# A four-layer attention kernel: the last layer's last block attends with block-diagonal operands on TensorE, and the order is searched anew

## The chip, the cores and the metric

The kernel runs on one core of a Trainium2 chip. The metric is the device time of one execution in microseconds; lower is better. Besides the times there is one profiled execution, whose trace lists every instruction of TensorE (PE, with its weight loads as PEld), VectorE (DVE), ScalarE (ACT), GpSimd (POOL) and the DMA issues of SyncE (SP).

## The reference

The input is `x` of 2048 tokens by 512 channels, in bf16. Four residual layers follow one another, A, B, A, B, with the same weights for both A and for both B layers. Each normalizes `x`, attends with 32 heads of 16 channels, projects and adds to `x`.

```python
def _A_ref(x, wqkv, w_phi, wo):                 # linear attention
    ...
    phi_q = jnp.concatenate([_softmax(pq, axis=-1), _softmax(-pq, axis=-1)], axis=-1)
    phi_k = jnp.concatenate([_softmax(pk, axis=-1), _softmax(-pk, axis=-1)], axis=-1)
    kv = jnp.einsum("bhsf,bhsd->bhfd", phi_k, v)
    ...
def _B_ref(x, wqkv, wo):                        # dilated window
    W, dil = 8, 2
    ...
    idx = pos[:, None] - off[None, :]           # off = 0, 2, ..., 14
    ...
    logits = jnp.einsum("bhsd,bhswd->bhsw", q, kg) * scale
    logits = jnp.where(mask[None, None, :, :], logits, -1e9)
    attn = _softmax(logits, axis=-1)
    o = jnp.einsum("bhsw,bhswd->bhsd", attn, vg)
...
x = x + _A_ref(_layernorm(x, axis=-1), ...)
x = x + _B_ref(_layernorm(x, axis=-1), ...)
x = x + _A_ref(_layernorm(x, axis=-1), ...)
x = x + _B_ref(_layernorm(x, axis=-1), ...)
```

In a B layer a token attends to itself and to the seven tokens 2, 4, ..., 14 places before it. Even tokens therefore see even tokens only, and odd ones odd.

## The kernel before

The tokens are cut into four blocks `b` of 512, and each block into four tiles `t` of 128. `x` stays in SBUF for all four layers (`x_83` to `x_86` in the profile are blocks 0 to 3). A class `_Fast` holds one method per stage; a method does not issue instructions but appends steps (closures) to threads, one thread for each stage and engine.

What sets the order of all engines is a list written out in the file: `_ORDER` names one thread after another, and `run` takes the next step of that thread. So the order of each engine's instructions is fixed by hand (by a search done beforehand), and each engine runs its own list strictly in order. `_CHOICE` has one bit for each PSUM eviction or similar step that could run on DVE or ACT (`flex`): 1 puts it on DVE. `_SLOTS` gives for each buffer that is asked for the slot it gets: 8 `big` ones (8 KB per partition), 16 `med`, 6 `t2`, and the 8 PSUM banks `ps`. `_OPT` holds options, among them `tr_dma`, the (layer, block) pairs whose normalized `x` is transposed by a DMA rather than by PE.

Stages of an A layer: `s_a1` (keys and values, softmax features, the sum `kv`), `s_a2` (queries), `s_akv`, `s_a3` and `s_a4` (normalization, output, projection with `WoA`, residual). `s_norm` does the normalization; it casts (`xn`, DVE L444 or ACT L446) and transposes (`xnT`, PE L460 with an eviction, or a DMA).

Stages of a B layer, for each block:

- `s_b1`, 48 matmuls 128x512 at L927: queries, keys and values transposed, channels on partitions. The values, with a halo of 16 tokens, are copied by 16 DMAs into `Vg`, which holds shifted copies of them.
- `s_b2`: four DVE products (L1019, `prod`, 128x4096) of the queries with eight shifted views of the keys. 32 matmuls with a 0/1 matrix (L1026, 128x32 tiles) sum them over the channels into logits. ACT takes two exponentials of 128x512 (L1033). Two matmuls (L1042) sum the denominators, ACT inverts them (L1047, L1049), and DVE normalizes (`PT`, L1054).
- `s_b3`: four DVE products (L1081, `pav`, 128x4096) of the probabilities with `Vg`, and 32 matmuls (L1090) that sum them. In the blocks 2 and 3 of the last layer the last product is split into two halves. ACT or DVE evicts to `oT` (L192, L190).
- `s_out`: four 128x512 matmuls per tile with `WoB` (L520), and the residual, added by DVE (L533) or by PE with the identity (L523) and then an ACT copy (L530). In the last layer SP then stores the tile (L544).

At the end `s_flag` counts whether all sums of exponentials (`stE`, 16 columns) and of reciprocals (`stR`, 8 columns) are within bounds. If not, a general path computes everything again.

Of the kernel before, what the change touches and what calls it, by code (L numbers as in the profile page):

```python
# [8 lines left out]
BF16 = mybir.dt.bfloat16  # L9
# [21 lines left out]
VGW = 3 * KVW + TB + 8  # L31
FRO2_MAX = 2.9
# [25 lines left out]
av 8 i i i i i i i i i i i i 0 f 0 g e 2t 0 bs 9 h a d c 0 j k t i i j l 27 o p 3 3 d6 b 1x 1x t 1y o m 2 2 1q  # L58
1z 1x 1x q u t r 1q v x w n s 1r w 1s 4 20 y 21 1x 22 1x 23 1q 1q 1q 1q 1v 1w z 3d 3d 3d 1u 1t 25 3e 3e 3e z 5
3e 3e z z 26 10 18 18 d5 1 z 16 11 4i 15 6 1h 13 3d 3e 3e 25 25 26 18 25 18 12 26 26 28 26 26 26 26 19 12 28  # L60
2a 28 1h 18 14 12 12 1a 28 1c 3e 2g 2g 1f 2h 2h 1h 1h 1b 1i 2b 1b 1e 1d 29 2j 2k 1h 1j 1n 2r 1b 1l 2s 1b 2c 2r
1k 2s 17 2g 2g 2h 2h 1k 1k 2h 2h 2h 2h 2d 1g 2d 2d 2d 2e 2j 1m 35 36 32 2o 2o 33 2s 33 32 33 33 2r 2s 2s 1o 2o
2o 2d 2r 3a 1k 3a 1p 2p 2o 24 24 2s 24 2u 2v 35 37 2u 2u 2u 2s 2i 2w 2j 3a 2s 3a 2l 2z 2j 24 32 32 34 2m 3b 33
3d 3f 3f 2z 2z 2z 33 2f 33 33 2f 2f 2f 3a 3a 2q 2q 2q 30 3a 2n 3a 3a 2z 3e 2q 2x 35 35 b6 3b 3a 2y 31 31 31 31
3c 3c 38 3c 39 3c 3m 3f 3n 3o 3o 3o 24 24 3g 3g 3g 3f 3p 3q 3g 3g 3g 3g 3g 3r 3q 3f 3g 24 3h 3i 3i 5l 5m 5n 3p
3s 3q 3j 3k 3k 3t 3q 3p 3x 5m 3w 3u 3h 3i 3i 3q 3v 3q 3q 3y 3h 3i 3q 3i 3h 3i 3q 5l 5o 5p 5r 5m 5q 7 7 3z 3q
3i 3j 3k 5m 5l 5s 3k 7 7 5m 5m 5m 3h 3i 7g 40 5u 44 41 42 5t 5m 5m 3j 3j 7h 7i 3k 5v 5m 5w 43 7h 45 7j 45 60
3k 3k 3k 46 45 45 5y 5x 5z 61 61 48 47 47 61 49 47 4a 47 4b 62 47 4b 63 3j 4g 94 4c 45 4d 45 4e 4f 3k 45 45 61
64 63 4h 4p 65 95 7j 7j 66 4q 63 96 95 97 97 63 67 7h 63 67 69 7h 6b 4k 4k 4k 4l 4p 4r 4k 4m 4p 4p 4s 4t 7k 7n
6a 68 6c 4o 7m 50 50 4u 4u 4u 4n 4u 7l 4w 97 7o 7p 7p 7q 7s 3l 4x 7r 7r 7p 7t 7p 6o 7u 50 7r 7r 7v 6o 6j 4v 4y  # L70
4j 6o 6q 6o 4j 4z 6k 6p 6r 6j 7r 6e 6l 95 6d 95 7v 6t 6s 6f 6d 7w 6e 7z 7x 98 9b 9a 99 6g 7y 9c 6e 6j 6j 9d 9d
6u 9d 6e 6n 80 6m 9d 6h 6v 6v 9e 9h 9f 6i 9g 9f 6w 6v 6v 6w 6w 9f 9i 9f 87 88 8h 9j 9f 50 82 9j 9l 6w 6x 6x 87
87 6w 81 83 9n 6x 9k 87 8b 89 51 51 51 51 52 52 8c 8c 8e 6u 6u 6u 9m 8j 8a 8d 8c 6v 6y 3l 8f 82 9o 82 85 82 50
51 52 4z 4z 4z 9q 9q 9s 8c 6z 8g 6y 6z 9r 71 70 6y 6y 6z 6z 72 86 a0 a0 a1 73 84 8i 74 75 74 74 50 74 8i 76 8i
77 a2 76 79 53 53 54 55 54 a5 56 53 54 9v 78 76 9q 9q 76 a0 81 53 9v 9w 9p 7a 57 9v 9u a7 76 7a 9t 8j 7c 9y 54
58 59 59 59 9v 59 9x 7d 7e 5a 8j 8j 7b 7f 5c 5b 5d 5b 5b a0 8k 5e 5b 5f 8k 9z a7 5b 5f 5j 8k 8k 8l a3 5i b4 a4
b7 5h b4 b4 b4 8l 5g b5 b5 a7 b5 b5 a7 8k 8l 8j c3 8i c3 b8 c4 c4 c4 c4 a8 8m a8 a8 a8 c3 a9 a9 5k at c1 b5 a6
8m au au c1 c2 b5 c2 aw c2 c2 a8 a9 b5 b5 8n 8o 8n 8p 8m at au at at 8n 8q 8m a7 aa 8n aw 8r 8s au au au 8s 8s
8t au au 8s 8v a6 a6 8u aa 8w aa 8x 8u 8u 8u 8y ab ac ab ad a6 aa b7 8u b9 b7 c3 8y 90 92 c1 91 c1 c2 8z c2 c2
aw ay ab c2 ba ae ab af aw b0 c4 c4 b1 bc ag ag ag ag ah bc aj ak bc c1 c4 c4 bc al ax c3 ai ai ai bd b1 ai am  # L80
93 bf bi bg az bf ai am ar bf bf bg bg aq b7 bg bg bg bg bg bb an ao ag ag ap bi ag ag b1 b1 bc b2 c2 bi bn bi
bl bk as bq br br bq br br bq bq b1 br by by by by bt b3 b3 b3 b3 br be be be br br bz c5 c5 bh bj bn bn bn c5
bu c4 by by by by c6 bo by c6 c6 c5 bt bt bt bn bv c6 c6 c6 bz be bp bp bw bm bp bp c0 c0 by c6 c6 bx c0 c0 c9
c5 ca c6 cb cb cc cb cd ce cd fr fs c7 c8 c7 c8 c8 ft cc ci cf cd cg cd c7 c8 c8 fs fu c8 e2 fu ch cd e3 cd cc
cj ck e4 cd c7 c8 c8 c7 e3 e2 cm cd c8 e6 e7 fu cl cd cd cn cp co e5 e3 hb e3 cr e2 ea e9 cq hc cs e3 cs e8 e3
e3 hd eb ec e3 e3 e3 ed ct cv hc eh cs he ee cs ef cw eg ei cx ei ei cu ei cu cu cu fs cy fs fv ej cu cy d0 cz
ek d2 fw fx fz d3 cs cs fy cs cs g0 g0 g0 el ek em ek en ek d4 d1 dc g1 eo ek g2 g3 g2 dc de eo es g0 g4 dd dh
g2 g5 g2 he hc eq g6 d7 d8 d7 d7 d7 he di dc g2 dc d9 ep er hc et dn hf da db df dh dh dh hi hh hj hg hk hk hk
dj dk dl dm dm g6 g7 g9 dn dn dg ga f0 f0 hl hm hn hm ho hm ev ew f1 hk dn g8 do do hp f2 fa fc hm hq do do dp
ev ex fc gb ev f0 dp ey dn f3 f0 hm fc f4 hq ev ez fc do dp dn dq dq d6 f5 f6 dm dm eu hs gi gj gi fd gs hr fd  # L90
ht fd hu hv fd dq fe fe f5 f5 f8 f5 f9 f7 fb gk fd fe fc gn gn gp gi gi gl gm gd gd gd ge ic gf i7 i7 i9 gg i8
dr dr dt ds dr du hx hy gd dq gu dr dv gn gq gh i7 ff ia gu fb go ff fg fh fb fb eu gv gc gn i2 gr i3 hx hz hx
i7 i2 ib gv i4 hx i1 gc hw i2 i2 i5 gu i0 gu gv gv gw gt ie fg fi if i6 ie id gw if dw dx id gv gw id id ie ie
if if ig dw ff ig if ig fg fj dw e0 dw ff fg fk ie fl fm fl fn gu fl fl fp ih ih ih ih e1 ii ii ii ik ij fq dy
gt gt gt fo fo il io io io io ii im ip iq ip is ir ir ih ii in ip ip iu it ir gx ir gy gx gx gx gz gy h0 dz dz
iv gy h1 h4 gx gy h2 h4 iw iv h5 h5 h6 h7 gy h4 h3 h5 h8 h9 h7 h7 h4 h5 ha h7
# [4 lines left out]
    "0011111111111001110111111010000010010000000000000001011111101100100000110101000110000010000001110111"  # L101
    "1101011110010000110101000000000000001101011000000000100100000000000000000101111100000011011000000000"
    "0000000000001101111010000000100101011111010000011001110111000000000000000111111011101110010100101000"
    "00000000000001111001000000000000000000000000000000000000000000000000000000000001111"
# [25 lines left out]
class _Fast:  # L130

    def __init__(self, ctx, tc, A_x, A_wqkv, A_w_phi, A_wo, B_wqkv, B_wo, out):
# [15 lines left out]
        self.ntile = {t: 0 for t in _BUFS}  # L148
        for n in ("xn", "xnT", "oT", "Eq", "rS", "kvp", "K", "QT", "Vg", "PT", "vh"):
            setattr(self, n, {})  # L150
# [7 lines left out]
    def ps(self, dt=F32):  # L158
        return self.psp.tile([P, 2048 // (4 if dt == F32 else 2)], dt, name="ps", tag=self.slot("ps"))
# [35 lines left out]
    def constants(self):  # L195
        nc, const = self.nc, self.const
        self.ident = ident = const.tile([P, P], BF16, name="ident")
# [12 lines left out]
        self.maskE = const.tile([P, 2, 16], BF16, name="maskE")  # L210
        nc.gpsimd.memset(self.maskE[:], 1.0)
        for g in range(4):
            sl = self.maskE[32 * g:32 * g + 32, :, :]
            nc.gpsimd.affine_select(out=sl, in_=sl, pattern=[[8, 2], [1, 16]],
                                    compare_op=ALU.is_ge, fill=0.0, base=2 * g - HALO, channel_multiplier=0)
        self.kvT = const.tile([P, D], BF16, name="kvT")
        self.ZM = [const.tile([P, 8 * H], BF16, name="ZM%d" % i) for i in range(2)]
        for z in self.ZM:
            nc.gpsimd.memset(z[:], 0.0)
        self.R = const.tile([P, 8, H], BF16, name="R")  # L220
        self.stE = const.tile([P, 16], F32, name="stE")
        self.stR = const.tile([P, 8], F32, name="stR")
# [1595 lines left out]
```

## Time and profile before

| | us |
|---|---|
| median of 3 runs (lowest to highest) | 330.87 (330.28 to 331.13) |
| profiled execution, first to last instruction (span) | 327.5 |
| PE busy | 310.3 (95%) |
| DVE busy | 302.2 (92%) |
| ACT busy | 279.3 (85%) |
| POOL busy | 25.3 (8%) |

Of the profiled execution only the span is recorded, not a time of its own; the median is 3.4 us longer than the span, which is what lies around it. "Busy" is the time in which at least one instruction of the engine was under way. In rows of instructions the columns are the line of the kernel, engine, operation, output and inputs with their shapes and count, then busy time in us and the mean duration of one in ns, then idle time of the engine just before them. In timelines they are start and duration in us.

### The profile page before, as it was taken

The page shows a single profiled execution, that of the slowest core. Times are in us where ns is not written, and L with a number is a line of the kernel's source. Part 1 is how long each engine was busy: PE and PEld are TensorE (multiplying, and loading weights), DVE is VectorE, ACT ScalarE, POOL GpSimd, SP SyncE. Part 2 cuts the span into 40 slices and gives each one's busy share as a digit, 9 for nine tenths or more (in the row PEclk, how much of TensorE's full clock was granted, in tenths as well). Part 3 has the DMA queues.
Part 4 walks back from the last instruction along what each step waited for, and adds up shares of the span by engine and source line. Part 5 has one row for each costly group of instructions (what it writes and reads, how often), then busy time and mean ns, then how long its engine had stood idle before and what let it go on. Part 6 is the DMA issues. An engine that isn't in the chain of part 4 may idle for free. (4 is left out here: it accounts for less than half of the span.)

```text
span 327.5 us, 8033 instructions
## 1 busy us (share of the span) xinstructions
PE 310.3 (95%) x3176; PEld 149.5 (46%) x3203; DVE 302.2 (92%) x439; ACT 279.3 (85%) x634; POOL 25.3 (8%) x50
## 2 busy tenths in 40 slices
PE   7999999999999999999999999979999999999873
PEld 3655456445444444443444455644544454433221
DVE  7998995998998999899999999699999999999993
ACT  5999988998888999989999999798999996676550
POOL 4000000000021003000000000000000208400000
PEclk9999999999999999999999999999999999999999
DMA  7980000004556899998750300023436977679952
GB/s 197 380 197 3 0 2 4 2 20 120 105 148 135 152 164 133 139 121 154 137 135 1 67 3 2 4 59 90 128 58 125 179 146 134 150 139 158 166 176 92
DMA packets 37388, 35.41 MB, mean 108 GB/s; under 512 B 23008, under 2 KB 32224, under 8 KB 37344
## 3 DMA queue, kind: packets, MB, share of 16 engines
q1 hardware_dynamic: 36816, 34.81, 53.6%
q8 instruction: 27, 0.44, 0.6%
q14 instruction: 17, 0.14, 0.2%
q10 hardware_dynamic: 528, 0.02, 0.1%
HBM read 10.50 MB, written 2.36 MB: 39 GB/s over the span
## 5 line engine op out<-in xcount | busy, mean ns | idle before, releaser
L927 PE MATMUL ps<-xnT,WB 128*128 128x512 bf16 x384 | 87.6, 380 | 0.5 <-DMA xnT<-xn 0.5
L1081 DVE TENSOR_TENSOR pav<-PT,Vg 128x4096 bf16<-128x4096 bf16 (+1 forms) x34 | 72.0, 2162 | 1.5 <-DMA Vg<-V 1.0
L1019 DVE TENSOR_TENSOR prod<-QT,K 128x4096 bf16<-128x4096 bf16 x32 | 72.5, 2291 | 0.3 <-ACT QT L192 0.2
L927 PEld LDWEIGHTS <-WB 128*128 128x128 bf16 x384 | 42.3, 114 | 43.3 <-issue 5.8
L520 PEld LDWEIGHTS <-oT 128*128 128x128 bf16 x256 | 23.8, 97 | 34.5 <-ACT oT L192 5.7
L192 ACT CAST oT<-ps 128x512 bf16<-128x512 f32 (+1 forms) x60 | 32.1, 587 | 8.4 <-PE ps L1090 7.1
L706 ACT ACTIVATE Eq<-ps 128x512 bf16<-128x512 f32 x64 | 34.0, 615 | 0.7 <-PE ps L698 0.6
L520 PE MATMUL ps<-WoB,oT 128*128 128x512 bf16 x122 | 32.1, 380 | 2.4 <-ACT oT L192 2.0
L599 ACT ACTIVATE Ek<-ps 128x512 bf16<-128x512 f32 x64 | 33.6, 622 | 0.4 <-PE ps L593 0.2
L698 PE MATMUL ps<-xnT,WA 128*128 128x512 bf16 x128 | 30.7, 380 | 0.6 <-DVE Eq L816 0.6
L540 ACT ACTIVATE sqd<-x 128x512 bf16<-128x512 bf16 x48 | 30.1, 643 | 1.0 <-DVE x L533 0.8
L605 PE MATMUL ps<-WA,xnT 128*128 128x512 bf16 x120 | 30.0, 380 | 0.5 <-issue 0.2
L593 PE MATMUL ps<-WA,xnT 128*128 128x512 bf16 x124 | 29.7, 380 | 0.6 <-DMA xnT<-xn 0.2
L520 PE MATMUL ps<-WoA,oT 128*128 128x512 bf16 x120 | 29.2, 380 | 0.4
L533 DVE SCALAR_TENSOR_TENSOR x<-ps,x 128x512 bf16<-128x512 f32 x38 | 25.4, 686 | 1.9 <-PE ps L520 1.7
L192 ACT CAST V<-ps 128x512 bf16<-128x512 f32 x31 | 17.5, 595 | 4.4 <-PE ps L927 4.3
L192 ACT CAST K<-ps 128x512 bf16<-128x512 f32 x31 | 17.8, 585 | 3.7 <-PE ps L927 3.3
L530 ACT ACTIVATE x<-ps 128x512 bf16<-128x512 f32 x26 | 15.1, 598 | 6.4 <-PE ps L523 6.3
L192 ACT CAST QT<-ps 128x512 bf16<-128x512 f32 x29 | 17.1, 592 | 2.5 <-PE ps L927 2.5
L651 DVE TENSOR_TENSOR Ek<-Ek,rk 128x4096 bf16<-128x4096 bf16 (+1 forms) x10 | 18.6, 1858 | 0.5 <-ACT rk L646 0.5
L593 PEld LDWEIGHTS <-xnT 128*128 128x128 bf16 x128 | 12.1, 97 | 15.4 <-DMA xnT<-xn 0.7
L446 ACT ACTIVATE xn<-x,nmr,rstd 128x512 bf16<-128x512 bf16 x23 | 18.2, 822 | 1.0 <-DVE nmr L435 0.8
(129 smaller groups left out, 433.3 us busy)
## 6 DMA issues: line engine op xcount, KB each, us to landing
Vg<-V SPq DMA_DIRECT2D x128, 131.5 KB, 4.4
Prho<-rd SPq DMA_DIRECT2D x8, 512.0 KB
x<-in_A_x_dram SPq DMA_DIRECT2D x3, 512.0 KB
WB<-in_B_wqkv_dram SPq DMA_DIRECT2D x3, 512.0 KB, 11.6
wraw<-in_A_wqkv_dram SPq DMA_DIRECT2D x4, 256.0 KB, 4.5
out_dram<-x SPq DMA_DIRECT2D x4, 256.0 KB, 2.2
out_dram<-x SPq DMA_DIRECT2D x8, 128.0 KB, 2.2
x<-in_A_x_dram SPq DMA_DIRECT2D x4, 128.0 KB
```

What stands on the lines that cost most here:

```text
L192: self.nc.scalar.copy(out=out, in_=in_)
L520: nc.tensor.matmul(y[:], lhsT=oT[:, c, t * P:(t + 1) * P], rhs=Wo()[:, c, :], start=(c == 0), stop=(c == NB - 1 and not onpe))
L533: nc.vector.scalar_tensor_tensor(out=xb[:, t, :], in0=T[t][:], scalar=1.0, in1=xb[:, t, :], op0=ALU.mult, op1=ALU.add, **kw)
L540: nc.scalar.activation(out=sqd[:], in_=xb[:, t, :], func=ACT.Square, accum_out=T["ss"][:, t:t + 1])
L593: nc.tensor.matmul(pk[:], lhsT=xnT[:, t, k, :], rhs=self.WA[:, k, D:2 * D], start=(k == 0), stop=(k == NB - 1))
L599: nc.scalar.activation(out=T["E"][:, t, s, :], in_=T["k", t][:], func=ACT.Exp, scale=1.0 - 2.0 * s)
L605: nc.tensor.matmul(pv[:], lhsT=xnT[:, t, k, :], rhs=self.WA[:, k, 2 * D:3 * D], start=(k == 0), stop=(k == NB - 1))
L698: nc.tensor.matmul(pq[:], lhsT=self.WA[:, k, hb * P:(hb + 1) * P], rhs=xnT[:, :, k, :], start=(k == 0), stop=(k == NB - 1))
L706: nc.scalar.activation(out=self.Eq[L, b][s][:, :, hb, :], in_=T[hb][:].rearrange("p (t i) -> p t i", t=4), func=ACT.Exp, scale=1.0 - 2.0 * s)
L927: nc.tensor.matmul(pp[:], lhsT=self.WB[:, k, i * D + c:(i + 1) * D:NB], rhs=xnT[:, :, k, :], start=(k == 0), stop=(k == NB - 1))
L1019: nc.vector.tensor_tensor(out=pr[:], in0=QT[:, c:c + 1, :].to_broadcast([P, NW, TB]), in1=win, op=ALU.mult)
L1081: nc.vector.tensor_tensor(out=pv, in0=PT[:, :, lo:lo + n].unsqueeze(1).to_broadcast([P, NB, 2, n]), in1=vw, op=ALU.mult)
```

## The change

The change has three parts.

Block 3 of the last B layer (`EST = (1, 3)`) no longer goes through `s_b1`, `s_b2` and `s_b3`, but through the new stages `s_e0` to `s_e4`. POOL clears two big tiles `Qbd` and, once the A layers no longer need it, the weight tile `WA` and a tile `Vx`. The queries are projected as before, evicted to `Qs`, and scattered by 16 DMAs into `Qbd`, so that the heads lie block-diagonally. The values are projected with tokens on partitions, evicted with a column of ones for each head, written by three DMAs to DRAM and read back by twelve into block-diagonal chunks in `WA` and `Vx`, in pieces of 272 bytes. The last 64 tokens of block 2 are projected once more for keys (`hk`) and values (`hv`). For each tile and each parity of the tokens 16 to 24 small matmuls on 64x32 tiles of PE give the logits of 32 keys against 40 queries; ACT exponentiates them, DVE masks them (`et`), and 64 small matmuls on 128x32 tiles (`s_e3`) with the block-diagonal values give the output and the denominators. ACT inverts (two small instructions), DVE normalizes (`oB`), PE transposes, ACT or DVE evicts, and `s_out` follows as before.

Two more blocks, 2 and 3 of the first A layer, have their normalized `x` transposed by DMA.

`_ORDER`, `_CHOICE` and `_SLOTS` are written anew for the whole program; among other things the initial loads come in another order (`wraw` between the tiles of `x`). As before, block 2 is the last to finish in the last layer. PSUM becomes one tile `PS` of eight banks, from which `ps` takes one bank and `pp` two adjacent ones.

Counted in the two instruction lists: DVE has 4 `prod`, 3 full and 2 half `pav` and 1 `PT` less, and 4 masks (128x1280) and 4 `oB` (128x512 from PSUM) more. PE has 32 matmuls at L1026, 24 full and 16 half ones at L1090, 2 at L1042, 4 at L523 and 32 transposes less, and 144 logit, 256 output, 16 transposing, 16 `hk` and 4 `hv` matmuls more. SP has 16 `Vg` copies less and 31 new copies and 2 transposes more.

```diff
-    "tr_dma": (('B0', 1), ('B0', 2), ('B0', 3), ('A1', 0), ...
+    "tr_dma": (('A0', 2), ('A0', 3), ('B0', 1), ('B0', 2), ('B0', 3), ('A1', 0), ...
...
+    def s_e0(self):
+        def zq(i):
+            ...
+            self.Qbd[i] = self.big([2, NB, TB], "Qbd")
+            nc.gpsimd.memset(self.Qbd[i][:], 0.0)
+        def zv(i):
+            if i == 2:
+                self.Vx = self.big([7 * VCH], "Vx")
+                nc.gpsimd.memset(self.Vx[:], 0.0)
+            else:
+                nc.gpsimd.memset(self.WA[:, 2 * i:2 * i + 2, :], 0.0)
...
+    def s_e1(self, L, b):
...
+        def qsc(g, i):
+            lo = DH * g
+            nc.sync.dma_start(out=self.Qbd[i][lo:lo + DH, :, g % 4, :], in_=T[0][lo:lo + DH, 2 * i:2 * i + 2, :])
...
+        def vrd(r, j0, j1, c):
+            a = self.VD[L, b][64 * j0 + r:64 * j0 + r + 1, c * 8 * DV:(c + 1) * 8 * DV]
+            n = H * DV
+            src = bass.AP(a.tensor, a.offset, [[2 * n, 32], [64 * n, j1 - j0], [1, 8 * DV]])
+            ...
+            nc.sync.dma_start(out=dst, in_=src)
...
+    def s_e2(self, L, b, t):
...
+        def mm(S, g, c, r, s, n, pos, K, k0, q0):
+            ...
+            nc.tensor.matmul(out, lhsT=K[64 * g:64 * g + 64, c, k0 + r:k0 + 64:2],
+                             rhs=self.Qbd[c // 2][64 * g:64 * g + 64, c % 2, :, q0 + r:q0 + 2 * n:2],
+                             start=(s == 0), stop=(s == 1), tile_position=(64 * g, 32 * c), skip_group_check=True)
...
+        def ex(r):
+            ...
+            nc.scalar.activation(out=E, in_=T[r][:, :, 0:320], func=ACT.Exp, scale=float(DH) ** -0.5,
+                                 accum_out=self.stE[:, idx + r:idx + r + 1])
+        def msk():
+            E = self.ET[t][:].rearrange("p g s h q -> p (g s h) q")
+            nc.vector.tensor_tensor(out=E, in0=E, in1=self.maskW[:].unsqueeze(1).to_broadcast([P, 32, WN]),
+                                    op=ALU.mult)
...
+    def s_e3(self, L, b, t):
...
+            nc.tensor.matmul(T["O"][q:q + n, e, 0:NB * DV], lhsT=E[:, e // 4, ks, e % 4, pos:pos + n],
+                             rhs=self.chunk(r, j)[:, :, DV * e:DV * (e + 1)],
+                             start=(e % 4 == 0 and pos == 0), stop=(pos > 0),
+                             tile_position=(0, q), skip_group_check=True)
...
+        def nrm():
+            ...
+            nc.vector.tensor_tensor(out=out, in0=num, in1=T["r"][:].unsqueeze(3).to_broadcast([P, 8, NB, DH]),
+                                    op=ALU.mult)
...
     def stages(self):
...
+                if (L, b) == EST:
+                    self.s_e1(L, b)
+                    for t in (3, 0, 1, 2):
+                        self.s_e2(L, b, t)
+                    for t in range(4):
+                        self.s_e3(L, b, t)
+                    self.s_e4(L, b)
+                    continue
```

More of the change, by code (lines that the diff above doesn't have):

```diff
@@ L31 @@
 VGW = 3 * KVW + TB + 8
+WN = 40
+DV = DH + 1
+VCH = NB * 8 * DV
+EST = (1, 3)
 FRO2_MAX = 2.9
@@ L126 @@
+    "pp": (
+        "462462064646"
     ),
@@ L560, in s_out @@
         half = (key, b) in _OPT["half_ln"]
-        split = last and (1, b) in _OPT["split"]
+        split = last and lhs is None and (1, b) in _OPT["split"]
         if split:
@@ new lines, in s_e2, with sc @@
+    def s_e2(self, L, b, t):
+        nc, add = self.nc, self.step
+        st = "b2_%d%d" % (L, b)
+        idx = 14 + 2 * t
+        T = {}
+        def mm(S, g, c, r, s, n, pos, K, k0, q0):
+            o = S[32 * c:32 * c + 32, g, s * 160 + pos:s * 160 + pos + 1]
+            out = bass.AP(o.tensor, o.offset, [list(o.ap[0]), [WN, NB], [1, n]])
+            nc.tensor.matmul(out, lhsT=K[64 * g:64 * g + 64, c, k0 + r:k0 + 64:2],
+                             rhs=self.Qbd[c // 2][64 * g:64 * g + 64, c % 2, :, q0 + r:q0 + 2 * n:2],
+                             start=(s == 0), stop=(s == 1), tile_position=(64 * g, 32 * c), skip_group_check=True)
+        def sc(r):
+            S = T[r] = self.pp()
+            K = self.K[L, b]
+            for s in range(2):
+                k0 = t * P + 64 * s
+                for c in range(NB):
+                    for g in range(2):
+                        mm(S, g, c, r, s, 32 if t == 3 and s else WN, 0, K, k0, k0)
+            if t == 3:
+                for c in range(NB):
+                    for g in range(2):
+                        mm(S, g, c, r, 1, 8, 32, self.kvT[:, 0:256].rearrange("p (c i) -> p c i", c=NB), 0, 0)
+        def ex(r):
+            if r == 0:
+                self.ET[t] = self.med([2, 4, NB, WN], "et")
+            E = self.ET[t][:, :, 2 * r:2 * r + 2].rearrange("p g s h q -> p g (s h q)")
+            nc.scalar.activation(out=E, in_=T[r][:, :, 0:320], func=ACT.Exp, scale=float(DH) ** -0.5,
[4 more added lines that the diff above has]
+                                    op=ALU.mult)
+        for r in range(2):
+            add(st, "PE", sc, r)
+            add(st, "ACT", ex, r)
+        add(st, "DVE", msk)
@@ new lines, in s_e4, with pt, pe @@
+    def s_e4(self, L, b):
+        nc, add = self.nc, self.step
+        st, key = "b4_%d%d" % (L, b), "A%d" % (L + 1)
+        U = {}
+        def pt(t):
+            U[t] = self.ps()
+            for c in range(NB):
+                nc.tensor.matmul(U[t][:, c * P:(c + 1) * P], lhsT=self.oB[L, b][:, t, c * P:(c + 1) * P],
+                                 rhs=self.ident[:].rearrange("p (r q) -> p q r", r=2), start=True, stop=True)
+        def pe(t, dve):
+            if (key, b) not in self.oT:
+                self.oT[key, b] = self.med([4, NB, P], "oBT")
+            self.copy(dve, self.oT[key, b][:, t, :, :].rearrange("p c i -> p (c i)"), U[t][:])
+        for t in range(4):
+            add(st, "PE", pt, t)
+            self.flex(st, pe, t)
+        self.s_out("b3_%d%do" % (L, b), key, b, lambda: self.WoB, True,
+                   lambda t, c: self.oT[key, b][:, t, c, :])
```

287 lines of the change are left out of this document (216 added, 71 removed).

## The prediction

> **What bounds the kernel now.** I read the page's busy times and slices first, then the table of engines by stretch of time, then the timeline of the last 65 us, and last the groups by line and shape, for prices.
>
> ```profile
> span 327.5 us, 8033 instructions
> ...
> PE 310.3 (95%) x3176; PEld 149.5 (46%) x3203; DVE 302.2 (92%) x439; ACT 279.3 (85%) x634; POOL 25.3 (8%) x50
> ...
> PE   7999999999999999999999999979999999999873
> ...
> DVE  7998995998998999899999999699999999999993
> ```
>
> PE and DVE are both nearly full in almost every slice of 8.2 us. PE alone could not finish in less than 310.3 us with this work. What lies above that is 17.2 us of idle PE, and the question is who causes it and where.
>
> ```profile
> core 0: us, PE busy (x) PEld busy (x) DVE busy (x) ACT busy (x) POOL busy (x), PEclk, DMA share, GB/s
> ...
> 263.43:322.90 59.47, 54.07 (x391) 22.25 (x391) 58.49 (x41) 37.68 (x79) 10.26 (x5) 1.00 0.77 151
> 20.00:263.43 243.43, 237.98 (x2652) 116.82 (x2672) 226.12 (x344) 225.78 (x524) 10.69 (x17) 1.00 0.46 84
> ```
>
> ```profile
> 263.43 6.70 DVE L1081 TENSOR_TENSOR pav<-PT,Vg 128x4096 bf16<-128x4096 bf16 x3
> ...
> 300.72 16.70 DVE L1081 TENSOR_TENSOR pav<-PT,Vg 128x4096 bf16<-128x4096 bf16 x9
> ...
> 322.22 0.69 DVE L533 SCALAR_TENSOR_TENSOR x<-ps,x 128x512 bf16<-128x512 f32 x1 [0.35 <-PE ps L520]
> ```
>
> I cut at 263.43, where DVE begins the first output product (`pav`) of block 0 of the last layer, and end at 322.91, the end of the last residual. In these 59.5 us DVE is busy 58.5: it has no gap, so it alone sets the length of the stretch. PE is busy 54.07 and idle 5.4, mostly waiting for what follows from DVE's products. Ahead of the cut it is the other way round: from 20 to 263.43 PE idles 5.45 us in 243, DVE 17.3. The clock is 1.00 throughout. From 322.91 to the end of the span there are 4.6 us, the last stores and the program's end.
>
> **DVE.** The prices:
>
> ```profile
> L1019 DVE TENSOR_TENSOR prod<-QT,K 128x4096 bf16<-128x4096 bf16 x32 | 72.5, 2291 | 0.3 <-ACT QT L192 0.2
> L1081 DVE TENSOR_TENSOR pav<-PT,Vg 128x4096 bf16<-128x4096 bf16 x30 | 67.5, 2288 | 1.5 <-DMA Vg<-V 1.0
> L1081 DVE TENSOR_TENSOR pav<-PT,Vg 128x2048 bf16<-128x2048 bf16 x4 | 4.8, 1218 | 0.0
> L1054 DVE TENSOR_TENSOR PT<-E,rden 128x1024 bf16<-128x1024 bf16 x8 | 5.4, 687 | 0.0
> L816 DVE TENSOR_TENSOR Eq<-ps,Eq 128x512 bf16<-128x512 f32 x25 | 16.1, 682 | 0.1
> L816 DVE TENSOR_TENSOR Eq<-bs,Eq 128x512 bf16<-128x512 bf16 x7 | 2.9, 416 | 0.0
> L190 DVE COPY xnT<-ps 128x1024 bf16<-128x1024 bf16 x10 | 6.8, 686 | 0.7 <-PE ps L460 0.6
> L444 DVE TENSOR_SCALAR xn<-x,rstd,nmr 128x512 bf16<-128x512 bf16 x41 | 14.9, 408 | 0.4
> L533 DVE SCALAR_TENSOR_TENSOR x<-ps,x 128x512 bf16<-128x512 f32 x38 | 25.4, 686 | 1.9 <-PE ps L520 1.7
> ```
>
> Busy over count is the price of one in a dense run. Removed: 4 `prod` at 2.27 (9.1), 3 `pav` at 2.25 (6.8), 2 halves at 1.2 (2.4), one `PT` (0.7): 18.9. Added: four masks of 1280 elements, between `PT` with 1024 (0.68) and a half `pav` with 2048 (1.2), in proportion 0.81 each: 3.2; four `oB`, 512 elements from PSUM, at L816's 0.64: 2.6. The new choice of engines moves more to DVE than away: 4 residuals (2.7), 5 `xn` (1.8), net 3 casts (2.0, at the 0.67 of L533); the transposes by DMA save 4 copies of 0.68 (2.7), and 4 products now read SBUF and not PSUM (0.9 less). Net 10.2 less: DVE 292.
>
> Behind the cut, in the new order, DVE has 11 `pav`, 2 halves, 2 `PT`, one cast, 4 `prod`, 4 masks, 4 `oB`, 8 residuals and 1.0 of small flag work: 24.8 + 2.4 + 1.4 + 0.7 + 9.1 + 3.2 + 2.6 + 5.4 + 1.0 = 50.6, against 58.5 busy before. DVE is no longer the longest there.
>
> **PE.**
>
> ```profile
> L927 PE MATMUL ps<-xnT,WB 128*128 128x512 bf16 x384 | 87.6, 380 | 0.5 <-DMA xnT<-xn 0.5
> L1026 PE MATMUL ps<-prod,indQK 128*32 128x512 bf16 x256 | 16.4, 381 | 1.7 <-DVE prod L1019 1.7
> L1090 PE MATMUL ps<-pav,indAV 128*32 128x512 bf16 x240 | 16.1, 382 | 1.2 <-DVE pav L1081 1.1
> L460 PE MATMUL ps<-ident,xn 128*128 128x128 bf16 x112 | 8.9, 219 | 0.2 <-ACT oT L192 0.2
> L668 PE MATMUL ps<-Ek,vaug 128*33 128x64 bf16 x512 | 8.3, 194 | 0.0
> L714 PE MATMUL ps<-Eq,indS 128*32 128x128 bf16 x256 | 5.5, 221 | 0.9 <-ACT Eq L706 0.7
> L1090 PE MATMUL ps<-pav,indAV 128*32 128x256 bf16 x32 | 1.6, 278 | 0.0
> L1042 PE MATMUL ps<-E,indDen 128*128 128x512 bf16 x15 | 4.5, 379 | 0.0
> L808 PE MATMUL ps<-rho,indB 32*128 32x128 bf16 x128 | 4.3, 217 | 0.6 <-ACT oT L192 0.5
> ```
>
> Removed: 32 at L1026 (0.064 each, 2.05), 24 + 16 at L1090 (0.067 and 0.05, 2.4), 2 at L1042 (0.6), 4 at L523 (a full 512 column matmul like L927, 0.228: 0.9), 32 transposes (0.079, 2.5): 8.5. Added: 4 `hv` at 0.228 (0.9), 16 `hk` and 16 transposes of `oB` at no more than a transpose (2.5), 144 logit and 256 output matmuls. The trace has none of these last two. For the output ones (128x32 tiles, 68 columns, a weight load each) the nearest row is L668 (33 wide, 64 columns, a load each): 0.0162, together 4.15. For the logits (64x32 tiles, up to 160 columns with a stride) I take L714 (128 columns): 0.0215, 3.1. That makes 7.25; the ends are 400 x 0.0162 = 6.5 and, at L808's price, 400 x 0.034 = 13.6. Sum added 10.7, net +2.2: PE about 312.5.
>
> [...]
>
> Behind the cut the two lists of PE come out equal at these prices: 24 wide projections (5.5) have moved ahead of it, 16 of L1026, 40 of L1090, 2 of L1042 and 4 of L523 are gone (4.9), and `hk`, the transposes and the small matmuls have come (9.8); with the one wide group that straddles the cut that is a difference below 0.1 us. So PE keeps 54.1 us there, and the whole +2.2, less that, lies ahead: the cut comes 2.1 us later in PE's time, where PE is the limit.
>
> **ACT.** It gains eight exponentials of 640 columns.
>
> ```profile
> L1033 ACT ACTIVATE E<-ps 128x512 bf16<-128x512 f32 x16 | 9.5, 601 | 1.2 <-PE ps L1026 1.2
> ```
>
> At 0.6 for 512 columns, 0.75 for 640: 6.0, and two such fewer (1.2). With eight small instructions for the reciprocals, fewer residuals and fewer `xn`, the lists differ by about 2 us. Behind the cut ACT had 37.7 of 59.5, so this is covered by its slack of some 20 us; without that cover it would cost those 2.
>
> **SP, DMA and POOL.** Values now travel through DRAM, and SP runs its list in order.
>
> ```profile
> q1 hardware_dynamic: 36816, 34.81, 53.6%
> ...
> Vg<-V SPq DMA_DIRECT2D x128, 131.5 KB, 4.4
> ...
> 247.26 5.01 SPq L988 DMA_DIRECT2D Vg<-V  x8
> ...
> 267.41 40.52 SPq L988 DMA_DIRECT2D Vg<-V  x48
> ```
>
> SP issues one copy per 0.63 (5.01 / 8) to 0.84 us (40.52 / 48), and it lands 4.4 us later. The new list has 16 scatters for the queries, three writes of the values, 8 `Vg`, the 12 reads, then 16 `Vg` for block 2. The last value to be written (`hv`) is due some 10 us behind the cut (10 us of PE work lie before it). From there 3 + 8 + 12 issues and the landing are 18.9 us at 0.63 and 23.7 at 0.84, so the reads land at +28.9 to +33.7. PE's first output matmul has 31.5 us of PE work before it. I take no stall, and a bound of 2.2 on the one side. Queued behind that first matmul would be all of PE's remaining list, and with it the residuals. The scatters are issued within 10 to 13 us of the cut and land by +18; the first logits stand 19.6 us of PE work behind it: covered, narrowly.
>
> POOL clears five tiles of 3072 to 4096 columns, ahead of the V halo of block 2.
>
> ```profile
> 2.64 0.56 POOL L219 MEMSET ZM<- 128x256 bf16 x2
> ...
> 249.34 0.23 POOL L969 COPY vh<-V 128x64 bf16<-128x64 bf16 x1
> ...
> 272.97 2.30 POOL L969 COPY vh<-V 128x64 bf16<-128x64 bf16 x1
> ```
>
> A clear of 256 columns takes 0.28, so 4096 are at most 4.5 us and all five (18,144 columns) at most 20. POOL is idle for nine tenths of the time. Beside DVE's products its copies take 2.3 instead of 0.23, waiting for DVE and not the reverse, so I cost this at nothing; if clears held DVE, up to 20 us would come off DVE's slack of some 33 in the whole span.
>
> The start: the same loads in another order. PE's first wide matmul now needs the V columns of `WA`, which are issued after 1.5 MB and not 2.5. I put this at 0, with 1.3 either way.
>
> **The sum.** The cut at 263.4 + 2.1 = 265.5, less 0.5 that I allow for the relief of DVE ahead of it (bounds 0 and 2 of PE's 5.45 idle). Behind it PE is the longest: 54.1, 0.7 for the last residual, and 0.5 of idle (before: 5.4, nearly all behind DVE). End of the last residual 265.0 + 55.3 = 320.3, span 324.9, 2.6 shorter. The span lies 3.4 below the median of 330.87, so that is 328.3.
>
> **Rivals.** (1) Slower: PE waits at the first output matmul for the values' trip through DRAM. The reads come in 2304 pieces of 272 bytes. By the queue's row a packet takes 53.6% x 327.5 x 16 / 36816 = 0.076 us of an engine, so the reads are 10.9 us on all 16, on top of the `Vg` traffic at a share of 0.77. If the 8 `Vg` and the reads run one after the other at that rate, 3 + 8 issues at 0.84 (9.2), 10.9, doubled by the traffic beside it to some 16, and 4.4 make +39.6 against +31.5: 8 us of stall, and with the 2.6 gained 336; it is a loss from 2.6 us of stall on. A middle case is 333. [...] Chance 0.17. [...] Chance 0.08. (3) The relief of DVE is worth nothing, since the re-searched order idles elsewhere (the start, the layer norms): PE's 17.2 idle stays near 15, 330.9. For it speaks that PE was already 98% busy from 20 to 263. Chance 0.11. (4) It does not do what it says: one of the 22 and 11 counted columns fails its bound and the general path runs, hundreds of us. Chance 0.01.
>
> **Numbers.** The forecast has 0.63 and by itself a range of 324 to 330: costs at their low ends (0.75 on the small matmuls, 1.3 at the start, 1.5 more relief) give 324.8, and PE gaps of 2 instead of 0.5 give 329.8. The range of 323.9 to 333.6 takes in rival 3 and the middle of 1 and 2. A difference of 0.3%, 1 us, is about what a measurement of this kernel can tell. Faster by more is the forecast and the mildest part of rivals 1 and 2, 0.64; within it rival 3 and the 331 of rival 2, 0.13; slower the rest, 0.23.
>
> **What would show it.** DVE near 292, PE near 312 to 313, and behind the first `pav` of block 0 PE with gaps below 1 us while DVE has some 5. Right prices: the groups of logit and output matmuls near 3.1 and 4.2 us. Wrong: a stall of PE at the first output matmul with the reads as its releaser; DVE instructions lengthened while POOL clears; or the cut later than 266.

## The result and the profile after

| | us |
|---|---|
| before, median (lowest to highest of 4 runs) | 330.57 (330.07 to 331.13) |
| changed, median (lowest to highest of 4 runs) | 333.55 (332.85 to 336.35) |
| ratio, with its 95% interval | 1.0118 (1.007 to 1.0166) |
| changed, profiled execution: time, span | 336.35, 334.6 |

The change makes the kernel 3 us slower; the forecast was 2.6 us faster. The quotient of the two medians is 1.009, inside the interval of the ratio. The profiled execution is the slowest of the four; the spans of the other three are 331.1 to 332.5.

The page of the changed kernel, with its busy times, slices and queues:

```profile
span 334.6 us, 8823 instructions
...
PE 312.9 (94%) x3529; PEld 152.8 (46%) x3529; DVE 297.8 (89%) x445; ACT 280.9 (84%) x648; POOL 43.0 (13%) x64
...
PE   8999999999999998999999999889999999995982
...
DVE  5998996978989888999998899699699999999893
...
PEclk9999999999999999999999999999999999998997
...
q8 instruction: 29, 0.48, 0.7%
```

PE, at 9 nearly everywhere, has a hole in the slice that begins at 301.2 us (the 5 in the "5982" at its end; a slice is 8.4 us). The granted clock, 1.00 in both stretches of the kernel before, dips there too (the 8 in the row PEclk). The table of engines by stretch, cut as in the prediction at the first `pav` of block 0 of the last layer (now 271.17) and at the end of the last residual (329.01):

```profile
20.00:271.17 251.17, 242.57 (x2659) 118.15 (x2657) 227.35 (x356) 230.40 (x531) 18.05 (x19) 1.00 0.55 91
100.00:140.00 40.00, 36.64 (x258) 16.71 (x258) 36.60 (x34) 36.09 (x83) 6.36 (x5) 1.00 1.00 142
271.17:329.01 57.84, 51.90 (x739) 24.42 (x737) 55.25 (x44) 36.24 (x88) 18.58 (x9) 0.97 0.62 128
303.31:310.31 7.00, 3.45 (x9) 1.23 (x9) 7.00 (x4) 1.45 (x5) 0.00 (x0) 0.76 1.05 159
```

After the span and its length, the columns are PE, PEld, DVE, ACT, POOL busy, the clock, the DMA share and GB/s. Behind the cut PE is busy 51.9 of 57.84, and 3.55 of the missing 5.9 lie in one place, the last row, where the clock is 0.76 as well. Ahead of the cut PE idles 8.6 (before: 5.45), of it 3.36 between 100 and 140 (before: 0.16, from 39.84 busy of 40).

The timeline of the hole, PE and what stands beside it:

```profile
302.92 0.39 PE L543 MATMUL PS<-WoB,oT 128*128 128x512 bf16 x1
...
303.70 4.60 DVE L1348 TENSOR_TENSOR oB<-PS,rdB 128x512 bf16<-128x512 f32 x2
306.86 1.44 PE L543 MATMUL PS<-WoB,oT 128*128 128x512 bf16 x3 [3.56 <-issue]
...
308.10 0.63 PE L546 MATMUL PS<-x,ident 128*128 128x512 bf16 x1
...
308.52 1.78 PE L543 MATMUL PS<-WoB,oT 128*128 128x512 bf16 x4
...
310.36 1.03 PE L543 MATMUL PS<-WoB,oT 128*128 128x512 bf16 x4
```

PE stops after the first matmul of a group of four whose inputs are all there, right behind 128 output matmuls (`s_e3`), and goes on 3.56 us later. "issue" means that nothing the profile shows was waited for. Four matmuls at 308.52 take 1.78 where four at 310.36 take 1.03: the first four run at half clock. The trace's clock record has 0.5 from 306.63 to 310.04 and 1.0 on both sides.

Some of the groups of the new instructions:

```profile
L1348 DVE TENSOR_TENSOR oB<-PS,rdB 128x512 bf16<-128x512 f32 x4 | 9.2, 2497 | 1.3 <-ACT rdB L1340 1.3
...
L1303 DVE TENSOR_TENSOR et<-et,maskW 128x1280 bf16<-128x1280 bf16 x4 | 3.1, 822 | 0.0
...
L1321 PE MATMUL PS<-WA,et 128*8 128x68 bf16 (+1 forms) x152 | 3.0, 196 | 0.0
...
L1277 PE MATMUL PS<-Qbd,K 64*32 64x160 bf16 (+1 forms) x128 | 2.0, 233 | 0.0
...
L1178 PE MATMUL PS<-xnT,WB 128*128 128x64 bf16 x16 | 0.6, 193 | 0.0
```

The masks cost what was forecast (0.82 each), the small matmuls less, and `oB` 2.3 each (9.2 / 4) where 0.64 was forecast.

So there are two suspects in the tail: what stops PE at 303.31, and the price of `oB`. For the first, the trace also lists when the queues' packets moved. Queue 8, which the page calls "instruction", brings blocks of 16384 bytes. The stops counted further down lie 256 instructions apart; at 256 to a block, an estimate from them, its 29 packets make 7424, and PE's records number 7083. I take it for PE's instruction stream (the runs below with 140 or 252 instructions more on PE have 30 packets):

| packet of queue 8 starts | PE instructions started by then |
|---|---|
| 284.35 | 5807 |
| 293.66 | 6071 |
| 303.71 (lands 305.24) | 6593 |
| 309.90 | 6609 |

The packets before these came 133 to 376 instructions after one another, and 248 to 264 between 247 and 294 us; here 522 went by between two packets. 256 of them were the 128 output matmuls and their weight loads, in 1.8 us; as many instructions of wide matmuls take 29 us (128 at 0.228, the price of L927). **Theory S (supply)**: PE ran out of instructions. **Theory D**: `oB` lengthens the tail, and PE's gap is its shadow. **Theory O**: the new order idles elsewhere, in 100 to 140 above all, and the tail is not the point.

### The profile page after: what moved, and what is told of

It reads as the page before. It is cut to its first block, busy times and chain, and to the rows that moved or that the text cites. A ratio compares the mean times of both kernels' runs of the same rounds, so it can differ in the third digit from the quotient of the medians.

```text
span 334.6 us, 8823 instructions
## 1 busy us (share of the span) xinstructions
PE 312.9 (94%) x3529; PEld 152.8 (46%) x3529; DVE 297.8 (89%) x445; ACT 280.9 (84%) x648; POOL 43.0 (13%) x64
## 4 chain that ended last, share of the span: by engine, by line
PE 30%; ACT 21%; DVE 12%; DMA 10%; issue 5%; SPq 0%; DVEq 0%; ACTq 0%
PE PS L950 12%; PE PS L543 6%; ACT Eq L729 5%; DMA xnT<-xn 4%; ACT sqd L563 4%; DMA Prho<-rd 3%; ACT Ek L622 3%; DVE prod L1042 3%; PE PS L1049 2%; PE PS L1170 2%; DVE pav L1104 2%; PE PS L1113 2%; DMA Vg<-V 2%; DVE Ek L674 2%; DMA out_dram<-x 2%
## 5 line engine op out<-in xcount | busy, mean ns | idle before, releaser
L950 PE MATMUL PS<-xnT,WB 128*128 128x512 bf16 x336 | 77.3, 380 | 0.9 <-DMA xnT<-xn 0.5
L1042 DVE TENSOR_TENSOR prod<-QT,K 128x4096 bf16<-128x4096 bf16 x28 | 63.2, 2285 | 0.3
L622 ACT ACTIVATE Ek<-PS 128x512 bf16<-128x512 f32 x64 | 34.0, 626 | 0.4 <-issue 0.4
L729 ACT ACTIVATE Eq<-PS 128x512 bf16<-128x512 f32 x64 | 34.2, 621 | 0.0
L543 PE MATMUL PS<-WoB,oT 128*128 128x512 bf16 x112 | 29.2, 394 | 3.8 <-issue 3.6
L205 ACT CAST oT<-PS 128x512 bf16<-128x512 f32 (+1 forms) x50 | 27.2, 593 | 6.5 <-PE PS L1113 6.4
L721 PE MATMUL PS<-xnT,WA 128*128 128x512 bf16 x128 | 30.6, 380 | 0.3 <-DVE Eq L839 0.3
L628 PE MATMUL PS<-WA,xnT 128*128 128x512 bf16 x128 | 30.7, 379 | 0.1
L543 PE MATMUL PS<-WoA,oT 128*128 128x512 bf16 x128 | 30.8, 380 | 0.0
L616 PE MATMUL PS<-WA,xnT 128*128 128x512 bf16 x128 | 30.7, 379 | 0.0
L556 DVE SCALAR_TENSOR_TENSOR x<-PS,x 128x512 bf16<-128x512 f32 x42 | 27.1, 683 | 0.8 <-PE PS L543 0.7
L205 ACT CAST K<-PS 128x512 bf16<-128x512 f32 x31 | 17.6, 595 | 2.5 <-PE PS L1170 1.9
```

The source lines that it names most:

```text
L205: self.nc.scalar.copy(out=out, in_=in_)
L543: nc.tensor.matmul(y[:], lhsT=lh(t, c), rhs=Wo()[:, c, :], start=(c == 0), stop=(c == NB - 1 and not onpe))
L556: nc.vector.scalar_tensor_tensor(out=xb[:, t, :], in0=T[t][:], scalar=1.0, in1=xb[:, t, :], op0=ALU.mult, op1=ALU.add, **kw)
L616: nc.tensor.matmul(pk[:], lhsT=xnT[:, t, k, :], rhs=self.WA[:, k, D:2 * D], start=(k == 0), stop=(k == NB - 1))
L622: nc.scalar.activation(out=T["E"][:, t, s, :], in_=T["k", t][:], func=ACT.Exp, scale=1.0 - 2.0 * s)
L628: nc.tensor.matmul(pv[:], lhsT=xnT[:, t, k, :], rhs=self.WA[:, k, 2 * D:3 * D], start=(k == 0), stop=(k == NB - 1))
```

## Experiments

Ratios are to the kernel before, run beside them on the same chip.

### More instructions ahead, same work

```diff
-            nc.tensor.matmul(self.warm_ps[:], lhsT=self.kvT[:, 0:P], rhs=self.kvT[:], start=True, stop=True)
+            nc.tensor.matmul(self.warm_ps[:, 0:432], lhsT=self.kvT[:, 0:P], rhs=self.kvT[:, 0:432], start=True, stop=True)
+            for _ in range(5):
+                nc.tensor.matmul(self.warm_ps[0:32, 0:16], lhsT=self.kvT[:, 0:32], rhs=self.kvT[:, 0:16], ...)
```

This is the run with 140 instructions more. The run with 252 has 368 columns in place of 432, and 9 small matmuls in place of 5.

> Theory S (supply): in the changed kernel PE stood still for 3.56 us at 303.31 because it had run out of instructions: 256 of them (128 matmuls with their weight loads) went in 1.8 us, and the next block of 16384 bytes on queue 8 only began to move at 303.71 and was in use at 306.86; after that PE ran 3.41 us at half clock, 1.7 us of work more. Rival D (DVE): the tail is longer because oB costs DVE 2.3 us each and not 0.64, and PE's gap is the shadow of that. Here each of the 14 warm-up matmuls of the start is cut into one of 432 columns and five of 16, the same columns in all: 140 instructions more before everything else, so that the block boundary falls in the middle of the first batch of output matmuls. S: the gap behind that batch falls below 0.7 us, the half-clock stretch is gone (mean clock near 0.998, not 0.989), and the time drops by at least the 1.35 us for which DVE waited behind the delayed second batch, at most by 3.56 + 1.7 = 5.3 us: 328.3 to 332.2, nearer to 332, because oB still fills DVE. D: gap and clock stay, 333.5 within 1 us.

> The same with nine small matmuls in each warm-up step (252 instructions more, nearly one whole block of 256), so that the boundary falls where it fell in the changed kernel. S: the stall of 2.5 to 4.5 us is back behind the first batch of output matmuls, with the half-clock stretch, and the time is 333.5 within 1 us; the pair of runs differs in the phase of the blocks alone. D: no difference to the run with 140.

Measured: 339.34 us (338.47 to 340.95), ratio 1.0285 [1.0259, 1.0312], and 342.06 (339.09 to 344.24), ratio 1.0335 [1.0287, 1.0383]. Both miss the expected times, which were 328.3 to 332.2 and 333.5 within 1. They are spoiled at the start: with the cut warm-up the clock record gives full clock only from 17.2 us (19.1 in the second run, 6.3 in the changed kernel), and the first wide projection of the first run comes at 17.62 instead of 10.98. I had not expected that. The tails can still be read. The waits between 296 and 320, with 140 and then with 252:

```profile
PEld L1367 <- DVE oB L1351: 2.2, 2, 1.9
...
PE PS L1367 <- DVE oB L1351: 1.6, 1, 1.6
```

```profile
PEld L549 <- issue: 3.0, 2, 2.7
PE PS L546 <- issue: 2.4, 1, 2.4
```

With 140 more, the stall behind the first batch is gone, and PE waits for `oB` instead; with 252 it is back (2.4). The half-clock stretch was to be gone with 140; it is there (314.19 to 317.61), but behind a wait for `oB` of 1.56. The stall itself fits S. Whether it is worth the time has to be asked without touching the warm-up.

### The price of oB

```diff
-            num = T["O"][:, :, 0:NB * DV].rearrange("p e (c d) -> p e c d", d=DV)[:, :, :, 0:DH]
-            out = self.oB[L, b][:, t, :].rearrange("p (d c e) -> p e c d", c=NB, e=8)
+            num = T["O"][:, :, 0:NB * DV].rearrange("p e (c d) -> p d c e", d=DV)[:, 0:DH, :, :]
+            out = self.oB[L, b][:, t, :].rearrange("p (d c e) -> p d c e", c=NB, e=8)
```

(and the reciprocals broadcast to match). In the second run only `out` is changed, to `"p (e c d) -> p e c d"`, which leaves out the order of columns that the output projection needs.

> The same four oB normalisations with their loops turned: written in order (contiguous), read from PSUM with strides; before, read nearly in order and written at every 32nd column. If the scattered write is what costs, oB falls from 2.3 to about 0.7 us, DVE by 6.4; if the read with strides costs as much, it stays at 2 or more. S: even at 0.7 the time drops only by 1 to 1.5 us (332.2), since PE's stall and its half clock stay. D: the time drops by 5 to 6.4 us, to about 328.

> The oB normalisation written in order and read in order: the columns of oB then stand in another order than the output needs, and nothing else is changed. The price of oB without any stride: 0.69 us by both theories (the price of 512 elements from PSUM); the time as in the run with turned loops, if that is cheap.

Measured: 332.71 us (330.04 to 336.3), ratio 1.0068 [1.0042, 1.0094], and 333.58 (331.46 to 334.26), ratio 1.0092 [1.0061, 1.0124]. The groups, of the turned loops and of the plain one:

```profile
L1349 DVE TENSOR_TENSOR oB<-PS,rdB 128x512 bf16<-128x512 f32 x4 | 3.9, 1016 | 4.1 <-ACT rdB L1340 4.1
```

```profile
L1348 DVE TENSOR_TENSOR oB<-PS,rdB 128x512 bf16<-128x512 f32 x4 | 2.7, 682 | 1.9 <-ACT rdB L1340 1.9
```

It was the scattered write: 2.3 with it, 1.0 with the scatter moved to the PSUM read, 0.68 with neither. DVE is 5 us shorter (293.0), but the kernel gains only 0.3 to 0.5% against the changed kernel's 1.0118, and the PE of the run with turned loops still stands for 3.44 at 302.77:

```profile
306.21 1.06 PE L543 MATMUL PS<-WoB,oT 128*128 128x512 bf16 x3 [3.44 <-issue]
```

DVE now waits 4.1 for the reciprocals of the delayed second batch. D falls as the whole cause: taking 5 to 6 us off DVE in the tail is worth a third of that at most (1.0118 less 1.0068 is 1.7 us).

### Both, with the warm-up left alone

```diff
             T["pb", s] = pb = [self.ps() for _ in range(4)]
+            for _ in range(35 if L and b < 2 and s == 0 else 0):
+                nc.tensor.matmul(pb[0][0:32, 0:16], lhsT=self.ident[:, 0:32], rhs=self.ident[:, 0:16], ...)
```

This is ahead of L831, in two waits of PE for `rho` (in the second A layer, not in the last layer as the first expectation says); 35 makes 140 instructions more, 63 makes 252. The second and third run also have the turned loops of `oB`.

> The 140 instructions more (70 tiny matmuls with their weight loads, into a bank that is overwritten afterwards) now stand in two waits of PE for rho in the last layer (0.75 and 0.84 us long at 213.9 and 220.8 in the changed kernel), so that the warm-up of the start is as in the changed kernel. S: no gap over 0.7 us behind the first batch of output matmuls; but oB at 2.3 us each then shows as waits of PE for oB, as in the run with 140 at the start (1.56 and 1.57), so the time drops by 1 to 2 us against the changed kernel: a ratio to the kernel before of 1.004 to 1.009. If the price of oB were no matter (PE alone sets the end): 5.3 us less, a ratio of 0.996. D: 1.012, nothing moves.

> The same 140, and oB with its loops turned (1.0 us each). Both causes taken away: stall and half clock gone, waits for oB gone. S: 3.4 of stall and up to 1.7 of half clock come off the 332.7 of the run with turned loops alone: 327.6 to 329.3, a ratio to the kernel before of 0.993 to 0.998. Rival O (order: the new order idles elsewhere and the tail's gains are given back by DVE): not below 331.

> The same with 252 instructions more in the same two waits and turned loops: almost a whole block, so the boundary is back where it was. S: the stall of 2.5 to 3.5 us is back and the time is that of the turned loops alone, 332.7 within 1. O: the same as the run with 140.

| | oB as in the change | oB with turned loops |
|---|---|---|
| no instructions added | 1.0118 [1.007, 1.0166] | 1.0068 [1.0042, 1.0094] |
| 140 added | 1.0105 [1.0069, 1.0142], 333.47 us | **0.9919 [0.9898, 0.9941], 327.84 us** |
| 252 added | not run | 1.0116 [1.0101, 1.013], 333.9 us |

Each remedy alone is worth 0.5% or less, which its interval does not separate from the changed kernel; the two together are worth 2.0%, well clear of it. The run with 252 was expected at 332.7 within 1 and misses by 0.2. The 140 and the 252 differ in 56 useless pairs, 1.4 us of PE (126 take 3.6 us, 70 take 2.2), and in 6 us of time. The tail of the run with both, from its cut at 269.09 to its last residual at 320.52, and of the run with 252:

```profile
269.09:320.52 51.43, 50.03 (x738) 24.18 (x737) 50.08 (x44) 36.19 (x88) 19.00 (x9) 1.00 0.68 138
```

```profile
270.32:326.33 56.01, 50.52 (x739) 24.31 (x737) 50.36 (x44) 36.30 (x88) 18.56 (x9) 1.00 0.64 129
```

1.2 of the 6 us is the later cut, the price of the pairs. Behind it the same work, 50 us each for PE and DVE, takes 51.4 in one and 56.0 in the other. The waits of the latter between 296 and 320 name the reason, a stall behind the first batch and another inside the second:

```profile
PE PS L543 <- issue: 2.7, 1, 2.7
DVE oB L1352 <- ACT rdB L1343: 2.5, 2, 1.3
...
PE PS L1324 <- issue: 1.5, 1, 1.5
```

The run with 140 and the dear `oB` missed its expectation of 1.004 to 1.009 a little, and its time alone does not tell S from D (1.012); its trace does. It has no stall, but three waits for `oB`, and a half-clock stretch (316.6 to 320.0) after them:

```profile
PE PS L1367 <- DVE oB L1351: 4.6, 3, 1.6
```

That is why neither remedy alone shows: with the stall gone PE waits 4.6 for `oB`, and with `oB` cheap it stalls for 3.4 and loses up to 1.7 to the half clock.

### The batch pulled apart

In `_ORDER` one word is moved: the second half of the first batch of output matmuls stands behind three groups of output projections more (turned loops).

```diff
- ... ii ii ga fi fj gr gr gr ij dw ij gr fj fj ij ij ik ik ...
+ ... ii ga fi fj gr gr gr ij dw ij gr fj fj ii ij ij ik ik ...
```

> Turned loops, no instructions added, but the second half of the first batch of output matmuls (64 with their loads) stands three groups of wide output projections later (3.2 us), so that the 256 instructions of the batch take 5.0 us and not 1.8. S: the next block needs some 6 us from the batch's start, so the stall falls from 3.4 to about 1 us and the time to 329 to 330.5. If the stall were a wait for one of the batch's own results, it would move with the half and keep its length.

> Turned loops, 140 instructions more, and the second half of the first batch moved three wide groups back. The run with the half moved alone had its stall inside the second batch (1.9 us at 310.24), so spreading did not make the blocks come sooner, only the want later. With 140 more nothing is short anyway: the time is that of the 140 with turned loops, 327.8 within 1, or up to 1 us longer, because the second oB comes later and PE waited 1.22 for oB in the run with the half moved.

Measured: 332.88 us (331.03 to 336.08), ratio 1.009 [1.0058, 1.0122], where 329 to 330.5 was expected; and with 140 instructions more 330.2 (327.62 to 333.21), ratio 0.9993 [0.997, 1.0016], where 327.8 within 1 was expected. Both miss. In the first the stall left the first batch, but it came back in the second, between two matmuls of the same batch:

```profile
310.03 0.20 PE L1282 MATMUL PS<-WA,et 128*8 128x68 bf16 x2
312.13 0.20 PE L1282 MATMUL PS<-Vx,et 128*8 128x68 bf16 x2 [1.90 <-issue]
```

The matmul behind the gap reads a tile of `et` and a block of values that the batch had read just before (at 310.02), and adds to a part of PSUM that the batch had begun to write; nothing there had data to wait for. The pull also costs PE another wait, 1.22 and 1.24 in the two runs, which the expectation puts down to `oB`. The trace names ACT's copies of `x`, which free the bank of PSUM:

```profile
308.00 1.24 PE L1325 MATMUL PS<-ident,oB 128*128 128x128 bf16 x8 [1.22 <-ACT x L514]
```

In ACT's list these copies stand behind the reciprocals of the moved half, for which ACT waits 3.47 and 3.32. In all the pull cost 2.4 us against the 140 without it.

### How far the boundary must move

The same with 16 and 32 pairs (32 and 64 instructions more), turned loops; one execution each.

> A finer test of the mechanism: 32 instructions more in the two waits for rho (turned loops). If PE holds two blocks of 256 and asks for the next one when it enters the second, then the stall is 5.5 us (from entering to use: 300.68 to 306.21 with turned loops alone) less what PE has left to do in the block it entered. With 32 more it enters that block 1.1 us earlier (299.57) and runs out 32 instructions earlier, in the middle of the batch: a gap of about 2.6 us, inside the batch of output matmuls or right behind it. By a rival in which the gap is a wait for data, it stays at 3.4 behind the batch.

> The same with 64: PE enters the block at 296.87, so the next is there at 302.4 and is wanted at 301.8: a gap of 0.3 to 0.6 us inside the batch, no half clock, and a span within 1 us of that with 140 more (326.4).

Measured: 331.41 us, span 329.7, with 32 more; 327.35, span 325.5, with 64. With 64 there is no gap of 0.3 or more in the batches, where 0.3 to 0.6 was expected, no half clock inside the run, and the span is within 1 us of 326.4 as expected; with 32 there is none either but a wait of 0.42 for the values, where 2.6 was expected. The packet that came at 303.07 with turned loops alone starts at 298.96 with 32 instructions more. That PE holds two blocks and asks for the next one when it enters the second was my supposition, from the 522 instructions between two packets of the changed kernel; no trace shows when PE asks, and neither run has the gap worked out from it. So the stall goes between 0 and 32 instructions and not between 32 and 64. The rival, a wait for data that would stay at 3.4, is refuted again. The span of the first is 4.2 longer for other reasons: 2.5 lie ahead of the cut (PE idles 3.07 between 100 and 140 in it, and 1.31 in the other), and 1.7 behind it, most of it in short waits of PE (2.3 against 0.9 of idle). With one execution each, the times alone show little.

The traces hold a sharper test of S. In the twelve profiled executions with the new stages, eight of PE's gaps over 0.9 us behind the cut have no releaser but "issue". The number of PE's instructions, as the trace records them, that had started before each gap is:

| run | PE stops at, for | instructions before | goes on after the last packet of queue 8 has landed |
|---|---|---|---|
| changed kernel | 303.31, 3.56 | 6593 = 25 x 256 + 193 | 1.62 |
| turned loops | 302.77, 3.44 | 6593 | 1.67 |
| plain `oB` | 301.67, 3.11 | 6593 | 1.61 |
| plain `oB` | 309.93, 1.05 | 6849 = 26 x 256 + 193 | 1.68 |
| 252 at the start | 310.43, 2.40 | 6849 | 1.49 |
| 252, turned loops | 303.06, 2.71 | 6849 | 1.53 |
| 252, turned loops | 310.51, 1.46 | 7105 = 27 x 256 + 193 | 1.60 |
| half moved, turned loops | 310.24, 1.90 | 6849 | 1.51 |

PE stops behind the first batch in some and inside the second in others, and for 1.05 to 3.56 us. But all eight counts are 193 past a multiple of 256, and PE goes on 1.5 to 1.7 us after a packet of queue 8 has landed. A wait for data would follow the data and not the count. So S holds for the stalls.

## Why the prediction was wrong

**The steps that held.** PE's work: 312.5 was forecast and 312.9 measured, of which 1.7 is the half clock (3.41 us at half speed), so 311.2 without it. ACT gained 1.6 (2 forecast), hidden. The values' trip through DRAM (rival 1) was in time: SP had issued the last read by 297.80, and the first output matmul waited 0.38, for the mask:

```profile
301.15 0.64 PEld L1321 LDWEIGHTS <-et 128*32 128x32 bf16 x20 [0.38 <-DVE et L1303]
```

POOL's five clears took 15.5 us (bound 20), and `pav` beside them kept its length (2.28 to 2.32). Idle of PE behind the cut was put at 0.5; with both causes taken away it is 0.60 in the profiled execution (320.52 less 0.8 of residual, less 50.03 and the cut), and the time is 327.84 where 328.3 was forecast for the change as it stood.

**The step that failed first: "0.5 of idle" behind the cut.** It was 5.14, and 1.7 went to the half clock. I had counted the small matmuls' time, and not that 400 of them with their loads are 800 instructions, and that 256 go in 1.8 us, where as many of wide matmuls take 29 (128 at 0.228). PE stood still for 3.56 us when 522 instructions had started since the last packet of queue 8 began (6071 to 6593). The next block came too late: its packet began 0.4 us after PE had stopped and took 1.5, and PE went on 3.15 us after the packet began. When PE had asked for it, the trace does not show.

**The second: `oB` at 0.64.** I took it from L816, a row with as many elements and in-order access. The diff showed an output at every 32nd column, and I did not price it. The term was 2.6 and measured 9.2; it alone explains DVE's 297.8 against 292 (293.0 with turned loops), and behind the cut 55.25 against 50.6.

**The third: 0.5 of relief ahead of the cut.** PE's idle there grew from 5.45 to 8.6. Rival 3 named this. That is not this one execution alone: in the three experiments with the same instructions ahead of the cut it is 7.2 to 8.8. But it is not steady: between 100 and 140 PE idled 3.36 in the changed kernel, and 0.94 to 3.36 in the experiments that leave the start alone, whose instructions there are the same. In the profiled execution a `pav` waits 2.13. The profile names PE as the releaser, but the instruction waits for copies of `Vg` as well, and SP, which issues them, was held by a transpose till 119.17:

```profile
114.55 4.62 SPq L473 DMA_TRANSPOSE xnT<-xn  x1
...
126.20 2.29 DVE L1104 TENSOR_TENSOR pav<-PT,Vg 128x4096 bf16<-128x4096 bf16 x1 [2.13 <-PE PS L950]
```

A copy issued right behind it, at 119.21, lands after 5.5 us in the median, at 124.7, and the next ones later, so either may have been last. I did not test which, nor what makes this idle time vary; it stays open.

**Sizes that cancelled.** A cut later than 266 was named as a sign of being wrong. It came at 271.17, not 265.0 (269.1 in the run with both remedies): 7.7 later than before, of which 4.6 is more work of PE ahead of it (242.57 less 237.98; 2.1 was forecast) and 3.15 more idle. PE's work behind it was 50.0 in the run with both remedies, not 54.1: 265.0 + 54.1 and 269.1 + 50.0 are the same 319.1. In part that is no accident, since work that moves from one side of the cut to the other leaves PE's total as it is. In part it is luck: PE's 312.6 in that run contain 2.2 of useless matmuls, and 312.5 was forecast without them. Logits cost 2.4 (2.0 and 0.4 in the groups) and not 3.1, the two output batches 1.7 and 1.1 and not 4.15. No run shows the price behind the 331 that the chances give to rival 2: the second batch has 128 matmuls in 1.14 us, 9 ns each, round four tile positions, and the 126 useless ones, all on one position, take 3.6 us, 29 ns each. And I added 3.4 from the span to the median; all later runs lie 1.7 above their spans, so before's profiled execution was simply a quick one. This shifts both kernels alike. In rival 1, 10.9 doubled is 21.8 and not 16; the reads came in time, so nothing hung on it.

## What to carry to other kernels

Where many tiny matmuls stand together, count PE's instructions as well as their time: here two packets of queue 8, 256 instructions each by the estimate above, never began to come less than 3.2 us apart in any run (4.06 at 290.02 and 294.08 in the run with both remedies), and the batches use 256 in 1.1 to 1.8 us. Price an elementwise step by its access pattern on both sides, and put the stride on the read if it must be somewhere: `oB` took 0.68 us in order, 1.0 with the stride on the read and 2.3 with it on the write. Two causes that stand one behind the other in the same stretch hide each other: neither of them alone gave back more than 0.5%, and both gave back 2.0%.

## What I had not expected of the hardware

- PE stops for want of instructions, for 3.56 us behind the first batch in the changed kernel and for 1.90 inside the second with the half moved, and the profile says only "issue". With turned loops, 140 useless instructions 80 us earlier remove the 3.44 us, and with 252 it is back (2.71 and 1.46).
- The half-clock stretches inside the runs are 3.41 us long (306.63 to 310.04 in the changed kernel, 314.19 to 317.61 with 140 at the start). The length of PE's gap does not decide whether one comes. Gaps of 3.56 and 3.44 us brought one, and gaps of 3.11 and 2.71 did not; but a gap of 2.40 did (252 at the start), one of 1.56 did (140 at the start), and so did waits of 1.44 and 1.56 close together (312.0 and 314.1, in the run with 140 and the dear `oB`).
- With the 14 warm-up matmuls cut into small ones, full clock came at 17.2 us (140 at the start) and 19.1 (252), against 6.3 in the changed kernel.
- 512 elements from PSUM on DVE: 0.68 in order, 1.0 with a strided read, 2.3 to 2.5 with a write at every 32nd column of two bytes.
